# A new explicit order for the first phase of a windowed-attention and feed-forward kernel

## The chip, the cores and the metric

The kernel runs on one core of one Trainium2 chip. The metric is the device time of one execution in microseconds, lower is better. The kernel before has a median of 850.51 us over three runs (849.96 to 850.99). About 0.2% of that (1.7 us) is what a measurement of this kernel can tell from no change.

## The reference

Eight batches of eight heads attend over 576 positions of 64 elements, each position to itself and the 63 before it; the result, laid out as 4608 tokens of 512 elements, goes through a two-layer feed-forward net with a leaky rectifier.

```python
scores = scale * np.matmul(q, k.transpose(0, 1, 3, 2))
mask = (rel >= 0) & (rel < 64)              # rel = query position - key position
scores = np.where(mask, scores, -1e9) - rowmax
attn = np.exp(scores) / (sum + 1e-09)
x = np.matmul(attn, v)                      # to (4608, 512)
h = x @ w_in                                # (512, 2048)
g = np.maximum(0.01 * h, h)
out = g @ w_out                             # (2048, 512)
```

The weights arrive as 64-bit floats; everything else is 32 bits.

## The kernel before, in words

Each product of the feed-forward net is made of three matmuls: a value is split into a rounded high part and the low part that is left, and high by high, high by low and low by high are summed. Scores are made transposed, keys on the partitions, so the maximum of a row runs across partitions, and GpSimd makes it with a PARTITION_ALL_REDUCE (line 332).

The program has two parts. The first is a list of names, `ORDER`, ahead of its `|`: each name is one step, and each step issues its instructions on its own engine in the order of the list. No scheduler moves them, so the list is the order of every queue. Everything behind the `|`, and all later work, is arranged by a planner in the program that the change does not touch. What the names do, with the line of the profile of before:

- TensorE: `X6` is six idle matmuls (503). `S0` makes the scores of block pair 0, in two banks; for pairs from 1 on it first writes the mask into the banks with two matmuls (312), then 64 small matmuls (278). `Z0` adds the mask to bank 0 afterwards. `N0` subtracts the maximum of bank 0 (346), `V0` multiplies the exponentials by the values (367), `T0` transposes a result (393), `M0` is a first product of the feed-forward net (431), `W0` the second product of the same job (467).
- GpSimd: `P0` to `P15`, one maximum for each bank (332).
- VectorE: `E0` and `E1` copy scores and mask from a bank to SBUF (322); `sub4` and later subtract a maximum (337); `sm`, `rec`, `y` are the sum, its reciprocal and the normalised result (374, 379, 386); `L` is the low part of x (401), `gl` that of the rectified h (445). `bits`, `sign`, `clamp`, `join`, `rest` (225, 229, 237, 242, 251) turn one 64-bit weight tile n into a high and a low part, with `abs` and `chi` (233, 245) on ScalarE between them. `bits`, `sign`, `clamp`, `join`, `rest`, `sub` and `gl` read SBUF alone; `sm`, `y` and `L` read a matmul bank.
- ScalarE: `E2` and later copy scores out of a bank (324), `exp` (351, 353), `H` is the high part of x (397), `lk` and `gh` are the rectifier and its high part (436, 441).
- DMA: `q`, `k`, `v` load a block pair's input on SyncE's queue (163, 167, 174); `raw` loads a weight tile (210), the first three on SyncE's queue and the others on ScalarE's. Weight tiles have three buffers, so `raw3` waits for `join0`.

A maximum can start when its scores are in SBUF and, from `P4` on, when the `sub` before it has read the maximum before. `M0` to `M10` are the products of the first 512 tokens, and each needs the low parts of x (`L`) and of its own weights (`rest`); `M1` needs `rest2`, `M2` needs `rest4`, `M3` needs `L3`, `W10` needs `rest15`. From `M11` on the weights are made already.

These lines of the program run the list:

```python
order, late = ORDER.split("|")
for name in order.split():
    step(name)()
```

Of the kernel before, what the change touches and what calls it, by code (L numbers as in the profile page):

```python
# [53 lines left out]
ORDER = """
q0 X6 S0 k1 raw0 q1 E0 P0 E1 bits0 sign0 raw1 v0 q2 k2 P1 X3 Z0 Z1 S1 abs0 E2 N0 exp0 X1 N1 bits1 sign1 abs1 clamp0
join0 clamp1 V0 sm0 join1 exp1 V1 E3 S2 chi0 raw2 chi1 raw3 rec0 sm1 rec1 bits2 sign2 y1 y0 P2 P3 N2 raw4 E4 rest1
rest0 E5 exp2 N3 exp3 T0 v1 V2 V3 k3 q3 abs2 H0 S3 v2 v3 q4 k4 sm2 P4 sub4 P5 rec2 sm3 L0 y2 rec3 clamp2 y3 exp4 V4 E6
T1 join2 H1 sub5 sm4 bits3 rec4 L1 exp5 X4 V5 P6 raw5 chi2 sign3 abs3 E7 bits4 rest2 sub6 sm5 clamp3 rec5 y4 y5 sign4
P7 M0 lk0 exp6 gh0 M1 abs4 gl0 T2 W0 join3 sub7 bits5 clamp4 V6 lk1 H2 exp7 raw6 L2 gh1 join4 V7 S4 chi4 raw7 chi3 gl1
sm6 sign5 sm7 rest4 rec7 rec6 rest3 M2 E8 abs5 y7 y6 T3 bits6 sign6 W1 lk2 H3 L3 clamp5 P8 M3 gh2 gl2 join5 v4 k5 q5  # L60
E9 S5 v5 q6 k6 raw8 lk3 gh3 chi5 abs6 sub8 bits7 exp8 gl3 M4 lk4 rest5 sign7 clamp6 W2 V8 P9 abs7 sub9 join6 gh4 raw9
M5 bits8 gl4 E10 sm8 sign8 exp9 chi6 W3 P10 clamp7 rec8 y8 join7 rest6 lk5 abs8 clamp8 gh5 V9 M6 W4 gl5 join8 bits9
sub10 sm9 sign9 rec9 y9 raw10 E11 raw11 chi7 P11 chi8 lk6 exp10 T4 gh6 abs9 rest8 rest7 bits10 M7 V10 W5 gl6 sign10
clamp9 H4 abs10 sub11 join9 L4 bits11 sm10 rec10 clamp10 y10 join10 lk7 raw12 exp11 gh7 gl7 S6 V11 chi9 rest9 sign11
W6 chi10 raw13 abs11 E13 E12 P12 rest10 sm11 bits12 clamp11 join11 rec11 y11 chi11 raw14 sign12 abs12 bits13 sign13
clamp12 sub12 join12 M8 T5 v6 q7 v7 k7 W7 lk8 gh8 H5 exp12 abs13 chi12 raw15 gl8 P13 bits14 L5 V12 sign14 clamp13
rest11 sub13 sm12 join13 rest12 rec12 S7 y12 E14 raw16 abs14 exp13 clamp14 join14 bits15 P14 W8 V13 M9 sub14 sm13
sign15 chi14 E15 exp14 chi13 abs15 lk9 gh9 P15 rec13 y13 V14 T6 rest14 rest13 sub15 M10 sm14 clamp15 gl9 rec14 join15
y14 exp15 raw17 H6 chi15 V15 W9 bits16 sign16 L6 lk10 gh10 abs16 raw18 sm15 rec15 gl10 y15 T7 H7 rest15 W10 clamp16
bits17 join16 sign17 L7 abs17 clamp17 join17 bits18 raw19 chi16 ev0 chi17 ev1 raw20 rest16 sign18 abs18 rest17 M11  # L70
bits19 clamp18 M12 lk11 gh11 gl11 lk12 gh12 sign19 join18 M13 W11 M14 gl12 abs19 raw21 chi18 lk13 bits20 clamp19
join19 chi19 raw22 sign20 rest18 rest19 W12 M15 gh13 gl13 abs20 W13 bits21 clamp20 sign21 join20 bits22 abs21 lk14
sign22 clamp21 join21 raw23 chi20 M16 gh14 gl14 W14 rest20 raw24 abs22 clamp22 join22 chi21 raw25 bits23 rest21 sign23
bits24 lk15 chi22 gh15 gl15 sign24 abs23 abs24 clamp23 join23 bits25 chi23 raw26 lk16 M17 W15 clamp24 sign25 rest22
join24 M18 abs25 gh16 raw27 clamp25 gl16 rest23 join25 W16 chi24 rest24 bits26 sign26 lk17 chi25 rest25 raw28 abs26
gh17 bits27 clamp26 gl17 sign27 join26 abs27 clamp27 join27 chi26 lk18 chi27 gh18 bits28 sign28 rest26 gl18 k8 q8 v8
W17 q9
|
abs28 raw29 clamp28 join28 bits29 raw30 sign29 rest27 abs29 bits30 chi28 clamp29 sign30 rest28 abs30 join29 clamp30
raw31 chi29 bits31 sign31 rest29 abs31 join30 clamp31 chi30 join31 rest30 chi31 rest31  # L80
# [1346 lines left out]
```

## Time and profile before

| | |
|---|---|
| median of three runs | 850.51 us |
| the profiled execution | 850.4 us, of it 848.6 us from the first to the last instruction |
| TensorE busy over the span | 841.8 us (99%) |
| VectorE busy from 20 to 80 us | 19.54, 19.70 and 19.12 of each 20 us |
| end of the first phase | about 140 us, where the planner's attention begins |

Times in the profile are in microseconds from the first instruction. Matmuls are pipelined and their ends are modelled, so a matmul's row may end later than the next begins. VectorE's instructions overlap by some 0.08 us, so a step of 0.42 us takes some 0.34 us of the queue. A row of the chain or timeline gives start, duration, engine, line, what is written and read, and the idle time before it.

### The profile page before, as it was taken

The numbers are of one execution on the slowest core, as the hardware profiler recorded it, in microseconds if no ns is written. First come the engines' busy times: TensorE is split into PE (matmuls) and PEld (weight loads), VectorE is DVE, ScalarE is ACT, GpSimd is POOL, SyncE is SP. The second block draws the span as 40 slices with busy tenths as digits, with TensorE's granted clock in tenths as the row PEclk, the third lists the DMA queues.
The fourth block names the chain that finished last, engine by engine and source line by source line (L and its number), as shares of the span: only waits on it lengthen the run. The fifth ranks groups of instructions, "written<-read, shape, count | busy, mean of one in ns | idle before, by whom it ended". The sixth has DMA issues, their size and how long they took to land.

```text
span 848.6 us, 16788 instructions
## 1 busy us (share of the span) xinstructions
PE 841.8 (99%) x6778; PEld 686.3 (81%) x6778; DVE 620.1 (73%) x883; ACT 375.7 (44%) x605; POOL 383.3 (45%) x218
## 2 busy tenths in 40 slices
PE   8999999999999999999999999999999999999998
PEld 5887888888878888888888888888888888888886
DVE  6999885748768779867649987585679955446863
ACT  4665654333433354454444433443354533324431
POOL 5422000878888715587587757857111111111110
PEclk9999999999999999999999999999999999999999
DMA  9875756798899869999999999999998986777682
GB/s 324 273 233 155 253 162 235 264 284 271 288 307 323 301 212 286 314 305 317 333 351 358 365 351 318 365 310 311 242 272 235 238 248 196 198 198 198 193 211 92
DMA packets 127757, 226.80 MB, mean 267 GB/s; under 512 B 15552, under 2 KB 46400, under 8 KB 127680
## 3 DMA queue, kind: packets, MB, share of 16 engines
q0 software_dynamic: 51552, 90.18, 38.4%
q10 hardware_dynamic: 35664, 77.31, 27.9%
q1 hardware_dynamic: 40464, 58.24, 21.1%
q8 instruction: 53, 0.87, 0.4%
q14 instruction: 24, 0.20, 0.1%
HBM read 172.52 MB, written 53.06 MB: 266 GB/s over the span
## 4 chain that ended last, share of the span: by engine, by line
PE 97%; DVE 2%; DMA 0%; ACT 0%; issue 0%; ACTq 0%
PE m L1118 27%; PE z L1181 18%; PE acc L929 11%; PE h L920 11%; PE y L1138 10%; PE h L431 5%; PE acc L467 5%; PE s L278 4%; PE o L740 4%; PE o L367 1%; DMA qk<-qk 0%; PE t L393 0%; DVE raw L225 0%; PE s L312 0%; DVE w L242 0%; DVE raw L229 0%
## 5 line engine op out<-in xcount | busy, mean ns | idle before, releaser
L1118 PE MATMUL m<-pfew,p 128*128 128x512 f32 x720 | 169.4, 391 | 0.0
L1118 PEld LDWEIGHTS m<-pfew,p 128*128 128x128 f32 x720 | 134.5, 188 | 28.3
L1102 POOL DMA_DIRECT2D p<-w_first x42 | 31.8, 757 | 113.4 <-PE m L1118 61.0
L929 PE MATMUL acc<-p,gs 128*128 128x512 f32 x324 | 80.6, 394 | 0.0
L1127 DVE TENSOR_TENSOR p<-m,pxa 128x512 f32<-128x512 f32 x60 | 41.3, 689 | 47.0 <-PE m L1118 46.0
L681 POOL PARTITION_ALL_REDUCE g<-late_f x20 | 36.8, 1875 | 78.7 <-DVE late_f L666 72.0
L684 POOL PARTITION_ALL_REDUCE late_o<-late_f x20 | 66.1, 3329 | 12.2 <-ACT late_f L692 7.0
L1118 PE MATMUL m<-pxb,p 128*128 128x512 f32 x288 | 70.9, 391 | 0.0
L1130 ACT ACTIVATE p<-p 128x512 f32<-128x512 f32 x60 | 37.9, 631 | 73.6 <-DVE p L1127 73.5
L929 PEld LDWEIGHTS acc<-p,gs 128*128 128x128 f32 x324 | 59.8, 188 | 12.8
L1127 DVE TENSOR_TENSOR pxa<-m,pxa 128x512 f32<-128x512 f32 x60 | 41.4, 690 | 35.4 <-PE m L1118 34.7
L684 POOL PARTITION_ALL_REDUCE late_o<-e x18 | 59.5, 3336 | 8.5 <-ACT e L692 3.6
L1118 PEld LDWEIGHTS m<-pxb,p 128*128 128x128 f32 x288 | 53.7, 188 | 11.3
L684 POOL PARTITION_ALL_REDUCE late_o<-late_e x18 | 59.3, 3322 | 5.5 <-ACT late_e L692 5.2
L1181 PE MATMUL z<-gs,p 128*128 128x512 f32 x240 | 57.6, 389 | 0.0
L920 PE MATMUL h<-pxa,p 128*128 128x512 f32 x228 | 54.9, 390 | 0.0
L1102 POOL DMA_DIRECT2D p<-w_second x28 | 22.7, 811 | 68.5 <-PE z L1181 31.0
L1181 PEld LDWEIGHTS z<-gs,p 128*128 128x128 f32 x240 | 45.0, 188 | 9.4
L1181 PE MATMUL z<-third,p 128*128 128x512 f32 x216 | 51.9, 389 | 0.0
L1181 PE MATMUL z<-pxa,p 128*128 128x512 f32 x216 | 51.9, 389 | 0.0
L920 PEld LDWEIGHTS h<-pxa,p 128*128 128x128 f32 x228 | 42.7, 188 | 9.0
L1102 POOL DMA_DIRECT2D p<-w_sums x16 | 12.0, 747 | 80.2 <-PE z L1181 55.8
(193 smaller groups left out, 1775.3 us busy)
## 6 DMA issues: line engine op xcount, KB each, us to landing
p<-w_first POOLq DMA_DIRECT2D x42, 1024.0 KB, 6.9
p<-w_second POOLq DMA_DIRECT2D x28, 1024.0 KB, 8.3
p<-w_sums POOLq DMA_DIRECT2D x16, 1024.0 KB, 5.7
qk<-qk ACTq DMA_DIRECT2D x26, 512.0 KB, 5.8
pspare<-w_second ACTq DMA_DIRECT2D x16, 512.0 KB, 7.2
w_sums<-pspare ACTq DMA_DIRECT2D x16, 512.0 KB, 7.7
raw<-w_out ACTq DMA_DIRECT2D x15, 512.0 KB, 3.9
raw<-w_in ACTq DMA_DIRECT2D x14, 512.0 KB, 3.9
```

What stands on the lines that cost most here:

```text
L431: nc.tensor.matmul(ps, a[:, k, :], b[:, k, part], start=n == 0, stop=n == len(terms) - 1)
L467: nc.tensor.matmul(acc[c, i], a[:, ts], b, start=begin and n == 0, stop=end and n == 2)
L681: nc.gpsimd.partition_all_reduce(most_of(j), e_of(m)[:, j], P, ReduceOp.max)
L684: nc.gpsimd.partition_all_reduce(sum_of(j), e_of(m)[:, j], P, ReduceOp.add)
L920: nc.tensor.matmul(ps, a[:, k, :], b[:, k], start=i == 0, stop=i == len(terms) - 1)
L929: nc.tensor.matmul(acc[c, i], a[:, i * P : (i + 1) * P], b, start=begin and k == 0, stop=n in ends and k == 2)
L1102: nc.gpsimd.dma_start(to, of, max_dma_last_dim=2048)
L1118: nc.tensor.matmul(tiles[b], w[:, 256 * i + 128 * kt : 256 * i + 128 * kt + 128], x_part(OF_X[k], j, kt), start=begin and c == 0, stop=c = ...
L1127: nc.vector.tensor_tensor(to(), tiles[b], x(), ALU.add)
L1130: nc.scalar.activation(to(), to() if b is None else tiles[b], AF.Prelu, alpha=0.01)
L1138: nc.tensor.matmul(tiles[i], a, b, start=f == 0 and k == 0, stop=f == FT - 1 and k == 2)
L1181: nc.tensor.matmul(tiles[b + i], a, x, start=begin and f == 0 and c == 0, stop=f == half - 1 and c == 2, skip_group_check=not begin,)
```

## The change

All 515 names ahead of the `|` are the same, in another order; nothing is added or removed. The list becomes one text line shorter, so each line of the program moves up by one. On GpSimd only `P2` and `P3` change places. The list's beginning shows the kind of change:

```diff
-q0 X6 S0 k1 raw0 q1 E0 P0 E1 bits0 sign0 raw1 v0 q2 k2 P1 X3 Z0 Z1 S1 abs0 E2 N0 exp0 X1 N1 bits1 sign1 abs1 clamp0
-join0 clamp1 V0 sm0 join1 exp1 V1 E3 S2 chi0 raw2 chi1 raw3 rec0 sm1 rec1 bits2 sign2 y1 y0 P2 P3 N2 raw4 E4 rest1
...
+X3 X6 q0 raw0 S0 E0 bits0 E1 sign0 q1 raw1 k1 S1 bits1 abs0 sign1 E3 clamp0 abs1 Z0 raw2 E2 P0 P1 clamp1 join0 N0 exp0
+P3 v0 q2 Z1 N1 k3 exp1 join1 V0 k2 raw3 sm0 S2 P2 rec0 chi0 y0 rest0 V1 N3 bits2 E4 chi1 P4 N2 q3 sm1 v1 raw4 rec1 v2
...
```

Three places matter to what follows. The first is SyncE's queue at the start, before (`qk` is q or k of pairs 0 and 1 with line 163 for q and 167 for k; `raw` is a weight tile, `p_1` holds q and k of pairs 2 and 3):

```order
L163 DMA qk_83<-qk 128x512
L167 DMA qk_84<-qk 128x512
L210 DMA raw_146<-w_in 128x1024
L163 DMA qk_84<-qk 128x512
L210 DMA raw_154<-w_out 128x1024
L174 DMA v<-vW 128x2x520
L163 DMA p_1_78<-qk 128x512
L167 DMA p_1_78<-qk 128x512
```

And the same place after the change:

```order
L162 DMA qk_83<-qk 128x512
L209 DMA raw_115<-w_in 128x1024
L162 DMA qk_84<-qk 128x512
L209 DMA raw_156<-w_out 128x1024
L166 DMA qk_84<-qk 128x512
L209 DMA raw_202<-w_in 128x1024
L173 DMA v<-vW 128x2x520
L162 DMA p_1_78<-qk 128x512
```

`k1` moves from second to fifth place, behind both first weight tiles, and `raw2` moves ahead of `v0`.

The second place is VectorE's queue from its first score copy to where `clamp` and `join` of the first two weight tiles stand, before:

```order
L322 SCALAR_TENSOR_TENSOR e<-s_0_111,p_0_77 128x512
L322 SCALAR_TENSOR_TENSOR e<-s_1_112,p_0_77 128x512
L225 TENSOR_SCALAR raw_146<-raw_146 128x512
L229 SCALAR_TENSOR_TENSOR raw_146<-raw_146 128x512
L225 TENSOR_SCALAR raw_154<-raw_154 128x512
L229 SCALAR_TENSOR_TENSOR raw_154<-raw_154 128x512
L237 TENSOR_SCALAR raw_146<-raw_146 128x512
L242 SCALAR_TENSOR_TENSOR w_213<-raw_146 128x512
L237 TENSOR_SCALAR raw_154<-raw_154 128x512
L374 TENSOR_SCALAR sm_225<-o_216 128x4
L242 SCALAR_TENSOR_TENSOR w_227<-raw_154 128x512
```

After:

```order
L321 SCALAR_TENSOR_TENSOR e<-s_0_117,p_0_77 128x512
L224 TENSOR_SCALAR raw_115<-raw_115 128x512
L321 SCALAR_TENSOR_TENSOR e<-s_1_118,p_0_77 128x512
L228 SCALAR_TENSOR_TENSOR raw_115<-raw_115 128x512
L224 TENSOR_SCALAR raw_156<-raw_156 128x512
L228 SCALAR_TENSOR_TENSOR raw_156<-raw_156 128x512
L236 TENSOR_SCALAR raw_115<-raw_115 128x512
L236 TENSOR_SCALAR raw_156<-raw_156 128x512
L241 SCALAR_TENSOR_TENSOR w_208<-raw_115 128x512
L241 SCALAR_TENSOR_TENSOR w_219<-raw_156 128x512
L373 TENSOR_SCALAR sm_233<-o_221 128x4
```

`bits0` moves ahead of `E1`, both clamps ahead of both joins, and `sm0` behind them.

The third place is VectorE's queue behind `sub5`, beside GpSimd's `P6`, up to `rest2` and `sub6`, before:

```order
L374 TENSOR_SCALAR sm_408<-o_389 128x4
L225 TENSOR_SCALAR raw_281<-raw_281 128x512
L379 RECIPROCAL sm_408<-sm_408 128x4
L401 TENSOR_TENSOR pxa_13_332<-t_399,pxa_12_331 128x4x128
L229 SCALAR_TENSOR_TENSOR raw_281<-raw_281 128x512
L225 TENSOR_SCALAR raw_295<-raw_295 128x512
L251 TENSOR_TENSOR pfew_85<-w_404,pfew_85 128x512
L337 TENSOR_TENSOR e<-e,g 128x512
```

After:

```order
L241 SCALAR_TENSOR_TENSOR w_407<-raw_202 128x512
L400 TENSOR_TENSOR pxa_13_375<-t_384,pxa_12_374 128x4x128
L224 TENSOR_SCALAR raw_297<-raw_297 128x512
L228 SCALAR_TENSOR_TENSOR raw_231<-raw_231 128x512
L373 TENSOR_SCALAR sm_440<-o_389 128x4
L373 TENSOR_SCALAR sm_442<-o_413 128x4
L378 RECIPROCAL sm_442<-sm_442 128x4
L228 SCALAR_TENSOR_TENSOR raw_297<-raw_297 128x512
L250 TENSOR_TENSOR pfew_85<-w_407,pfew_85 128x512
L336 TENSOR_TENSOR e<-e,g 128x512
```

`join2` now stands behind `sub5` (it stood ahead of it), `bits3` has gone ahead of this stretch, and `sm5`, `rec5` and `sign4` have come ahead of `rest2`. On TensorE the list begins with nine idle matmuls in a row, `X3 X6`, where `X6` stood ahead of `S0` and `X3` behind it; `S1` follows `S0` at once, and `Z0` and `Z1`, which stood ahead of `S1`, now stand each just ahead of `N0` and `N1`; `S2` stands between `V0` and `V1`, and `X1` has gone to behind `V2`.

More of the change, by code (lines that the diff above doesn't have):

```diff
@@ L54 @@
 ORDER = """
-q0 X6 S0 k1 raw0 q1 E0 P0 E1 bits0 sign0 raw1 v0 q2 k2 P1 X3 Z0 Z1 S1 abs0 E2 N0 exp0 X1 N1 bits1 sign1 abs1 clamp0
-join0 clamp1 V0 sm0 join1 exp1 V1 E3 S2 chi0 raw2 chi1 raw3 rec0 sm1 rec1 bits2 sign2 y1 y0 P2 P3 N2 raw4 E4 rest1
-rest0 E5 exp2 N3 exp3 T0 v1 V2 V3 k3 q3 abs2 H0 S3 v2 v3 q4 k4 sm2 P4 sub4 P5 rec2 sm3 L0 y2 rec3 clamp2 y3 exp4 V4 E6
-T1 join2 H1 sub5 sm4 bits3 rec4 L1 exp5 X4 V5 P6 raw5 chi2 sign3 abs3 E7 bits4 rest2 sub6 sm5 clamp3 rec5 y4 y5 sign4
-P7 M0 lk0 exp6 gh0 M1 abs4 gl0 T2 W0 join3 sub7 bits5 clamp4 V6 lk1 H2 exp7 raw6 L2 gh1 join4 V7 S4 chi4 raw7 chi3 gl1
@@ L60 @@
[L60 to L74, printed above, removed]
@@ L75 @@
-join24 M18 abs25 gh16 raw27 clamp25 gl16 rest23 join25 W16 chi24 rest24 bits26 sign26 lk17 chi25 rest25 raw28 abs26
-gh17 bits27 clamp26 gl17 sign27 join26 abs27 clamp27 join27 chi26 lk18 chi27 gh18 bits28 sign28 rest26 gl18 k8 q8 v8
-W17 q9
+X3 X6 q0 raw0 S0 E0 bits0 E1 sign0 q1 raw1 k1 S1 bits1 abs0 sign1 E3 clamp0 abs1 Z0 raw2 E2 P0 P1 clamp1 join0 N0 exp0
+P3 v0 q2 Z1 N1 k3 exp1 join1 V0 k2 raw3 sm0 S2 P2 rec0 chi0 y0 rest0 V1 N3 bits2 E4 chi1 P4 N2 q3 sm1 v1 raw4 rec1 v2
+y1 exp3 sign2 T0 V3 exp2 V2 rest1 sub4 X1 bits3 sm3 sm2 S3 E5 H0 rec2 exp4 y2 rec3 y3 L0 T1 V4 abs2 X4 P5 clamp2 sub5
@@ new lines @@
+join2 H1 L1 bits4 exp5 V5 E6 q4 sign3 raw5 M0 sm4 sm5 P6 rec5 chi2 E7 sign4 abs3 rest2 sub6 v3 rec4 clamp3 lk0 M1 gh0
+y5 P7 abs4 y4 clamp4 join3 gl0 k4 sub7 T2 exp6 V6 join4 raw6 W0 sm6 H2 exp7 bits5 L2 lk1 V7 chi3 sign5 chi4 rec6 raw7
+y6 sm7 S4 rest4 gh1 rec7 abs5 gl1 q5 E8 y7 M2 T3 clamp5 rest3 W1 P8 bits6 join5 H3 v4 lk2 chi5 k5 L3 sub8 sign6 M3 gh2
+gl2 raw8 exp8 V8 E9 bits7 sign7 P9 S5 abs6 clamp6 join6 lk3 raw9 gh3 q6 sm8 rec8 chi6 abs7 rest5 sub9 gl3 bits8 M4
+sign8 clamp7 lk4 W2 exp9 E10 abs8 join7 M5 y8 P10 gh4 clamp8 W3 raw10 gl4 lk5 gh5 chi7 rest6 join8 raw11 sub10 V9
@@ new lines @@
+bits9 W4 k6 sign9 gl5 E11 sm9 abs9 v5 rec9 rest7 chi8 y9 exp10 P11 clamp9 bits10 M6 T4 join9 H4 lk6 V10 rest8 W5 chi9
+sign10 raw12 abs10 sm10 sub11 bits11 sign11 abs11 L4 gh6 clamp10 join10 exp11 chi10 rec10 M7 raw13 gl6 y10 q7 S6 V11
+clamp11 rest9 E12 P12 join11 sm11 v6 bits12 W6 lk7 rec11 sign12 y11 chi11 gh7 rest10 E13 T5 sub12 M8 raw14 H5 exp12
+gl7 k7 V12 abs12 rest11 bits13 sign13 W7 lk8 clamp12 join12 sm12 rec12 L5 abs13 raw15 clamp13 gh8 chi12 bits14 P13
+sub13 sign14 gl8 abs14 S7 W8 join13 exp13 clamp14 raw16 rest12 E14 join14 v7 y12 bits15 V13 sign15 sm13 M9 P14 rec13
@@ new lines @@
+raw17 sub14 chi13 chi14 E15 abs15 rest13 exp14 y13 clamp15 P15 rest14 V14 T6 bits16 lk9 H6 join15 sub15 sm14 bits17
+sign16 gh9 rec14 M10 y14 gl9 L6 exp15 raw18 V15 chi15 abs16 sm15 rec15 W9 clamp16 lk10 join16 gh10 y15 T7 gl10 rest15
+sign17 raw19 H7 bits18 abs17 chi16 L7 sign18 clamp17 W10 rest16 abs18 join17 clamp18 raw20 M11 join18 bits19 sign19
+M12 v8 chi17 ev1 chi18 rest17 lk11 gh11 raw21 M13 gl11 bits20 ev0 abs19 lk12 clamp19 join19 M14 raw22 sign20 chi19
+abs20 W11 bits21 gh12 gl12 rest19 sign21 rest18 abs21 clamp20 lk13 join20 W12 clamp21 bits22 join21 gh13 gl13 raw23
@@ L78 @@
+chi20 lk14 sign22 raw24 M15 chi21 abs22 W13 rest20 clamp22 gh14 join22 gl14 chi22 M16 raw25 lk15 bits23 rest21 sign23
+bits24 sign24 abs23 gh15 abs24 rest22 clamp23 clamp24 gl15 W14 join23 bits25 chi23 join24 rest23 raw26 W15 sign25
+raw27 lk16 abs25 M17 chi24 gh16 clamp25 join25 chi25 gl16 raw28 bits27 rest25 bits26 sign26 sign27 lk17 rest24 gh17
+gl17 abs26 q9 clamp26 M18 join26 abs27 W16 clamp27 q8 chi26 join27 bits28 lk18 gh18 chi27 sign28 k8 rest26 W17 gl18
 |
```

## The prediction

> **What bounds the kernel now.** I read the page's busy times first, then busy time by stretches of 20 us, then the timelines of each engine through the first 40 us.
>
> ```profile
> span 848.6 us, 16788 instructions
> PE 841.8 (99%) x6778; PEld 686.3 (81%) x6778; DVE 620.1 (73%) x883; ACT 375.7 (44%) x605; POOL 383.3 (45%) x218
> ```
>
> ```profile
> 0.00:20.00 20.00, 17.95 (x290) 11.47 (x291) 13.54 (x24) 9.52 (x17) 9.70 (x9) 1.00 0.92 333
> 20.00:40.00 20.00, 18.98 (x335) 15.72 (x336) 19.54 (x50) 12.97 (x27) 8.82 (x5) 1.00 0.85 268
> 40.00:60.00 20.00, 20.00 (x225) 16.25 (x218) 19.70 (x43) 13.86 (x27) 5.17 (x3) 1.00 0.73 224
> ```
>
> The columns of the second fence are stretch, length, then busy time of TensorE's matmuls, its weight loads, VectorE, ScalarE and GpSimd. TensorE is full from 40 us on. So a microsecond won or lost before about 40 us goes straight to the end, as long as the later work is never late; and almost nothing can be won after it. VectorE is also nearly full there, 19.5 and 19.7 of 20 us. Before 40 us what TensorE does and waits for is this:
>
> ```profile
> 1.45 2.93 PE L503 MATMUL idle<-p 128*128 128x512 f32 x6 [1.45 <-DVE p L514]
> 4.74 1.98 PE L278 MATMUL s<-qk 64*64 64x64 f32 x64 [0.37 <-DMA qk<-qk]
> 6.66 0.97 PE L503 MATMUL idle<-p 128*128 128x512 f32 x3
> 24.43 1.70 PE L431 MATMUL h<-pxa,pfew 128*128 128x256 f32 x12
> 26.60 1.69 PE L431 MATMUL h<-pxa,pfew 128*128 128x256 f32 x12 [0.47 <-ACT g L436]
> 33.05 1.96 PE L431 MATMUL h<-pxa,pfew 128*128 128x256 f32 x12
> 35.05 0.63 PE L393 MATMUL t<-unit,y 128*128 128x128 f32 x4
> 36.90 1.77 PE L431 MATMUL h<-pxa,pfew 128*128 128x256 f32 x12
> ```
>
> The last five rows are M0, M1, M2, T3 and M3. M2 lasts 1.96 where M1 takes 1.69: it stands still inside for a weight's low part. What TensorE needs there comes from VectorE:
>
> ```profile
> 32.84 0.67 DVE L251 TENSOR_TENSOR pfew<-w,pfew 128x512 fp32r<-128x512 f32 x1
> 34.17 0.74 DVE L386 TENSOR_TENSOR y<-o,sm 128x256 f32<-128x256 f32 x2
> 36.34 0.69 DVE L401 TENSOR_TENSOR pxa<-t,pxa 128x512 fp32r<-128x512 f32 x1 [0.19 <-ACT pxa L397]
> ```
>
> These are rest4 (done 33.51, M2 began at 33.05), y7 and y6 (done 34.91, T3 at 35.05), and L3 (done 37.03, M3 at 36.90). So **VectorE sets the pace up to M3**, and TensorE alone after it. I judge the change by when VectorE has L3.
>
> **What a maximum costs VectorE.** GpSimd's first six maxima and some of VectorE's steps from SBUF beside them:
>
> ```profile
> 7.57 1.99 POOL L332 PARTITION_ALL_REDUCE g<-e  x1 [7.12 <-DVE e L322]
> 9.47 2.06 POOL L332 PARTITION_ALL_REDUCE p<-e  x1
> 11.43 2.07 POOL L332 PARTITION_ALL_REDUCE p<-p  x1
> 13.92 1.78 POOL L332 PARTITION_ALL_REDUCE p<-p  x1 [0.42 <-ACT p L324]
> 17.16 1.78 POOL L332 PARTITION_ALL_REDUCE g<-e  x1 [1.45 <-ACT e L324]
> 20.18 2.00 POOL L332 PARTITION_ALL_REDUCE g<-e  x1 [1.25 <-DVE sm L374]
> ```
>
> ```profile
> 8.92 0.69 DVE L229 SCALAR_TENSOR_TENSOR raw<-raw 128x512 uint32<-128x512 uint32 x1
> 9.54 1.31 DVE L225 TENSOR_SCALAR raw<-raw 128x512 uint32<-128x512 uint32 x1
> 13.93 1.58 DVE L242 SCALAR_TENSOR_TENSOR w<-raw 128x512 uint32<-128x512 uint32 x1
> 15.77 0.40 DVE L225 TENSOR_SCALAR raw<-raw 128x512 uint32<-128x512 uint32 x1
> 19.34 0.68 DVE L337 TENSOR_TENSOR e<-e,g 128x512 f32<-128x512 f32 x1
> 24.03 0.87 DVE L229 SCALAR_TENSOR_TENSOR raw<-raw 128x512 uint32<-128x512 uint32 x1
> 24.82 0.56 DVE L225 TENSOR_SCALAR raw<-raw 128x512 uint32<-128x512 uint32 x1
> ```
>
> A `bits` takes 0.40 alone and 1.31 when it starts 0.07 into a maximum; a `join` takes 1.58 against the 0.69 of the `sign` of equal size. So a step that starts at a maximum's beginning loses 0.9 us. The `sign` at 8.92 started 1.35 into the maximum that began at 7.57 and lost nothing. I take the price as what is left of the first 0.9 us of the maximum. Grouped by line, the steps from SBUF in the first 20 us (count, then busy time and mean ns of one):
>
> ```profile
> L225 DVE TENSOR_SCALAR raw<-raw 128x512 uint32<-128x512 uint32 x3 | 2.6, 871 | 0.0
> L242 DVE SCALAR_TENSOR_TENSOR w<-raw 128x512 uint32<-128x512 uint32 x2 | 2.3, 1134 | 0.0
> L251 DVE TENSOR_TENSOR pfew<-w,pfew 128x512 fp32r<-128x512 f32 x2 | 1.9, 972 | 0.0
> L237 DVE TENSOR_SCALAR raw<-raw 128x512 f32<-128x512 f32 x2 | 1.7, 874 | 0.0
> ```
>
> With 0.40 for a `bits` or `clamp` and 0.69 for the others their collisions come to 3 x 0.47 + 2 x 0.44 + 2 x 0.28 + 2 x 0.47 = 3.8 us.
>
> The Trainium skill, "SBUF — State Buffer", section "Who interferes with whom", says the same pair of ports is shared and that who comes second blocks fully, until the whole instruction of the first has ended. Here the trace differs: the join at 13.93 ended at 15.51, and its maximum at 15.70. By that rule each collision would cost up to 2.1 us, by the rows 0.9.
>
> **Part one, up to sub4.** The start: `X3 X6` puts three more idle matmuls ahead of S0. Six took 2.93 (with one modelled end in it), so three more take between 0.97 (the row of three at 6.66) and 1.5; S0 could have begun at 4.38 but for its input's 0.37. S0 begins at 5.4 instead of 4.74, near the lower end since the six hold one long last row; VectorE's E0 follows it, and the first maximum begins at 7.57 + 0.65 = 8.2. In the new order the five maxima can run without a gap, where before 0.42 and 1.45 were lost ahead of the fourth and fifth. At 1.9 to 2.05 each (start to start 9.47 - 7.57 and 11.43 - 9.47, with 0.1 to 0.2 when a VectorE step gets the memory first), five end at 18.2 to 18.6, and sub4 can start at 18.6 instead of 19.34. Two things must hold for that. VectorE must be there: it did the same steps (all but one `sm`) in 19.34 - 6.78 = 12.6 us before, (E0 started at 6.78, 0.1 behind S0's last row), of which 3.8 were collisions. That leaves 8.8, so from 7.4 on it has 18.6 - 7.4 - 8.8 = 2.4 us to lose. I find 2.3 to 3: `sign0` and `sign2` 0.3 to 0.5 each, `clamp0` 0.5 to 0.9, `join0` and `rest0` up to 0.8 each. And the inputs must be there:
>
> ```profile
> 2.12 0.43 SPq L163 DMA_DIRECT2D qk<-qk  x1
> 3.25 0.67 SPq L174 DMA_DIRECT2D v<-vW  x1
> ```
>
> ```profile
> qk<-qk SPq DMA_DIRECT2D x1, 256.0 KB, 6.1
> v<-vW SPq DMA_DIRECT2D x1, 520.0 KB, 7.6
> ```
>
> Before, q1 landed at 2.12 + 6.1 = 8.2 and v0 at 3.25 + 7.6 = 10.85; between them 512 KB of raw1 and 520 KB of v0, so 390 KB a microsecond. Now k1 is the last input of S1 and has raw1 ahead of it: 8.2 + 512/390 = 9.5. S1's small matmuls began at 9.01 and now begin at 9.5 to 9.6, done by 10.6. Its banks then go through E3 in 0.6, and the third maximum does not begin before 12.3, so the lateness is covered by 1 us; without cover it would cost 0.5. v0 lands at 12.2 and k2 at about 14.1, V0 and S2 start at about 13 and 14: just in time. **Term: -0.7 at sub4, from -1.0 to +0.3** (no gain, and the S1 lateness not covered to half).
>
> **Part two, from sub4 to L3.** VectorE is full, so what counts is the work ahead of L3 and the collisions. Counted in the new list, `clamp5` and `join5` have come ahead of L3 and `sign6` has gone behind: +0.42 (a clamp by the `bits` row's size). At P6 before, `sign3` (0.87 at 24.03) and `bits4` (0.56 at 24.82) lost 0.3 together; now E6, the score copy for P6, stands behind exp5 on ScalarE, P6 starts some 0.3 later, and `bits4`, `sign3` or `sign4` stand at its beginning: 0 to 0.9, I take 0.5, so +0.2. The 0.19 for which L3 waited on ScalarE before goes, since y6 and y7 now come ahead of `rest3`: -0.2. **Term: +0.4, from -0.3 to +1.2.**
>
> **Part three, from M3 to the end.** TensorE runs full. What could be late is the last weight of the first 512 tokens:
>
> ```profile
> 84.86 2.99 PE L467 MATMUL acc<-p,gs 128*128 128x512 f32 x12
> 83.42 0.68 DVE L251 TENSOR_TENSOR p<-w,p 128x512 fp32r<-128x512 f32 x1
> ```
>
> That is W10 and rest15, done 0.76 before W10 began. In the new list `bits17`, `clamp16` and `join16` come ahead of rest15, 0.34 + 0.34 + 0.6 = 1.3 us more. Against that, the `gl` steps stand later in VectorE's list, so the waits in front of them go:
>
> ```profile
> 66.44 0.86 DVE L445 TENSOR_TENSOR gs<-g,gs 128x512 fp32r<-128x512 f32 x1 [0.58 <-ACT gs L441]
> ```
>
> That one waited 0.58. With rest15's spare 0.76 this covers the 1.3: **term 0, up to +0.5**. All later work keeps its order, and starts sooner or later as a whole.
>
> **Sum.** -0.7 + 0.4 + 0 = -0.3. The profiled execution took 850.4, 1.8 more than its span, and lies at the median of the runs shown (850.51). Forecast: **850.1 us**, no change that can be told; its own range 849.0 to 851.4.
>
> **The rivals.** *A, the clock.* TensorE's matmuls are at half speed at first: S0's 64 took 1.98 us, the idle matmuls behind it 0.97/3 = 0.32 each against 0.49 at 1.45. Nine idle matmuls without the 0.37 gap could bring full speed before S0; then S0 takes about 1 us, the maxima begin 0.6 earlier and so may sub4: 850.1 - 0.6 = 849.5. Against it: full speed came only at about 7 us, after five microseconds of nearly steady work. The Trainium skill, "TensorE: Matmul & The Clock Gate", section "What's actually happening", states about 3.4 us of sustained work, in a window that does not start with the kernel; by that S0 could be fast here. *B, collisions gather (slower).* Between sub5 and L3 three steps stand where a maximum may just have begun: `sign3` at P6, `clamp3` behind `rec4` at P7, `gl1` at P8. At 0.9 each they cost 2.7, against 0.5 at these places before; with the 0.4 of extra work and no gain in part one VectorE has L3 2.6 late, less the 0.2: 850.4 + 2.4 = 852.8; with two of them and the gain, 851.2. It decides from the second collision on. For it: `clamp3` follows `sub6` by one short step only. Against it: a step right behind a `sub` can slip in first, as the next maximum starts 0.16 after the `sub` ends (sub4 at 19.34 + 0.68, P5 at 20.18). *C, no collision.* The new places dodge all of P6 to P8: part two becomes 0.4 - 0.5 - 0.2 = -0.3, and with -1.0 in part one and the fast S0 of A 850.4 - 1.9 = 848.5. *D, given back.* The gain of 0.3 is lost at W10, where VectorE is 0.5 late: 850.6.
>
> **How the numbers follow.** Forecast 47%, A 13%, B 17% (a third of it within 0.2%), C 15%, D 8%. Faster by over 0.2% needs 848.8: C and the edge of A and of the forecast, 0.22. Slower needs 852.2: most of B and the forecast's edge, 0.16. Within 0.2%: 0.62. The range must reach to C's time and into B's: 848.3 to 852.1.
>
> **What would show it.** Right: S0 at about 5.4, the first maximum at 8.2, five maxima without gaps, sub4 at about 18.6, M3 at 36.4 to 36.9, no TensorE wait from there to 140 us. Wrong: S1 waiting for k1 well past 9.6, gaps between the first maxima; `sign3`, `clamp3` or `gl1` at 1.2 us or more (B); all VectorE steps between sub5 and L3 at their plain durations (C); TensorE idle at W10 (D).

## The result, and the profile after

The changed kernel takes **855.57 us** (median of five runs, 855.13 to 857.58) against 850.36 for the kernel before on the same chip. The ratio is 1.0065, with a 95% interval from 1.0054 to 1.0077: 5.2 us slower, where no change was forecast, and 3.5 us above the range. The profiled execution is the longest of the five, 857.58, and the only one whose granted clock is below 1.000 (0.998). Its span is 7.2 longer than the one before, so some two of these 7.2 us belong to that execution alone; the section on the hardware shows 1.5 of them.

The page of the changed kernel, span and busy times:

```profile
span 855.8 us, 16780 instructions
PE 843.8 (99%) x6778; PEld 687.7 (80%) x6778; DVE 622.7 (73%) x883; ACT 374.7 (44%) x605; POOL 383.9 (45%) x218
```

TensorE is busy 2.0 us longer than before (841.8), with the same 6778 matmuls, and idle 5.2 us longer. Where, the stretches of 20 us say (columns as before: stretch, length, busy time of matmuls, weight loads, VectorE, ScalarE, GpSimd, then the granted clock, the DMA share and GB/s):

```profile
0.00:20.00 20.00, 15.87 (x263) 10.33 (x265) 11.78 (x22) 8.38 (x15) 10.07 (x9) 1.00 0.90 318
20.00:40.00 20.00, 18.82 (x295) 15.01 (x292) 19.67 (x48) 13.16 (x27) 7.94 (x4) 1.00 0.80 253
40.00:60.00 20.00, 17.95 (x185) 14.39 (x184) 18.27 (x37) 11.38 (x23) 6.39 (x3) 0.91 0.71 229
80.00:100.00 20.00, 19.16 (x125) 15.45 (x122) 18.46 (x40) 13.15 (x24) 3.13 (x2) 1.00 0.60 190
```

TensorE is busy 2.1 us less than before in the first 20 us (15.87 against 17.95), and is no longer full from 40 to 60 and from 80 to 100 us, where it was full before. On TensorE's timeline the steps that answer to those shown before are S0, M0, M3, M4, and two that wait now, T4 and V15:

```profile
5.69 1.16 PE L277 MATMUL s<-qk 64*64 64x64 f32 x64
25.88 1.69 PE L430 MATMUL h<-pxa,pfew 128*128 128x256 f32 x12
38.93 1.97 PE L430 MATMUL h<-pxa,pfew 128*128 128x256 f32 x12
43.20 1.70 PE L430 MATMUL h<-pxa,pfew 128*128 128x256 f32 x12
56.28 0.94 PE L392 MATMUL t<-unit,y 128*128 128x128 f32 x4 [2.04 <-DVE y L385]
88.14 0.69 PE L366 MATMUL o<-p,e 128*64 128x65 f32 x16 [0.83 <-ACT raw L232]
```

M0 comes 1.45 us later than before (24.43), M3 2.03 later (36.90). M4 is 3.0 later, of which 0.6 is V8, which stands ahead of it now; by M5 the delay is 2.44. T4 waits 2.04 for y9, V15 waits 0.83. V15's row names ScalarE's `abs` (232), which V15 does not read; it writes the bank that y14 has to empty first, and y14 ended at 87.99, 0.15 before V15 began, as y9 ended 0.15 before T4. From M11 on the delay is 7.14 to the end. What T4 waits for is on VectorE:

```profile
51.40 0.69 DVE L241 SCALAR_TENSOR_TENSOR w<-raw 128x512 uint32<-128x512 uint32 x1 [1.46 <-DMA w_single<-w]
53.07 0.69 DVE L228 SCALAR_TENSOR_TENSOR raw<-raw 128x512 uint32<-128x512 uint32 x1
53.68 1.26 DVE L444 TENSOR_TENSOR gs<-g,gs 128x256 fp32r<-128x256 f32 x1
55.14 0.66 DVE L250 TENSOR_TENSOR pfew<-w,pfew 128x512 fp32r<-128x512 f32 x1
55.72 0.42 DVE L385 TENSOR_TENSOR y<-o,sm 128x256 f32<-128x256 f32 x1
```

The first row is join8. It waits 1.46 us for a store to memory of an earlier joined weight (line 246), whose SBUF tile it is to overwrite. Before, the same wait was 0.19:

```profile
47.91 0.69 DVE L242 SCALAR_TENSOR_TENSOR w<-raw 128x512 uint32<-128x512 uint32 x1 [0.19 <-DMA w_single<-w]
```

Behind it come, in the change, sign9, gl5 (which meets the beginning of P11, 1.26 instead of 0.42), rest7, and only then y9. Behind T4's wait the granted clock falls, which the section on the hardware shows.

### The profile page after: what moved, and what is told of

It reads as the page before. It is cut to its first block, busy times and chain, and to the rows that moved or that the text cites. A ratio compares the mean times of both kernels' runs of the same rounds, so it can differ in the third digit from the quotient of the medians.

```text
span 855.8 us, 16780 instructions
## 1 busy us (share of the span) xinstructions
PE 843.8 (99%) x6778; PEld 687.7 (80%) x6778; DVE 622.7 (73%) x883; ACT 374.7 (44%) x605; POOL 383.9 (45%) x218
## 4 chain that ended last, share of the span: by engine, by line
PE 91%; DVE 4%; DMA 3%; issue 0%; ACT 0%; ACTq 0%; SPq 0%; DVEq 0%
PE m L1117 27%; PE z L1180 18%; PE acc L928 11%; PE h L919 10%; PE y L1137 10%; PE s L277 4%; PE o L739 4%; PE acc L466 3%; PE h L430 3%; DMA p<-qk 1%; DMA raw<-w_out 1%; DMA w_single<-w 1%; DVE raw L228 1%; DMA p<-eye_mask 1%; PE o L366 1%; DVE w L241 1%
## 5 line engine op out<-in xcount | busy, mean ns | idle before, releaser
L331 POOL PARTITION_ALL_REDUCE g<-e x13 | 26.8, 2065 | 50.7 <-ACT e L323 39.7
```

## The experiments

All experiments are other orders of the same 515 names. Letters of theories are used anew from group to group. The delays at M0, M5, S6 and W10 are those of the profiled execution against the profiled execution of before; the times are medians, each beside its own runs of before (850.3 to 850.6).

| kernel | M0 | M5 | S6 | W10 | us, median | ratio, 95% interval |
|---|---|---|---|---|---|---|
| the change | 1.45 | 2.44 | 6.18 | 7.12 | 855.57 | 1.0054 to 1.0077 |
| a_then_b | 1.49 | 1.44 | 1.44 | 1.44 | 852.24 | 1.0010 to 1.0029 |
| a_then_b_M5 | 1.21 | 2.20 | 2.46 | 2.46 | 853.16 | 1.0019 to 1.0044 |
| b_then_a | -0.05 | 1.88 | 3.08 | 3.94 | 854.30 | 1.0029 to 1.0060 |
| b_loads | 2.31 | 1.84 | 1.84 | 1.84 | 851.98 | 1.0006 to 1.0029 |
| b_v1 | 1.38 | 0.89 | 0.89 | 1.21 | 851.30 | 1.0001 to 1.0022 |
| a_loads | 1.94 | 2.55 | 3.37 | 4.18 | 855.58 | 1.0039 to 1.0069 |
| a_v1 | 1.64 | 2.63 | 3.85 | 4.66 | 855.16 | 1.0047 to 1.0072 |
| a_loads_v1 | 1.12 | 2.10 | 2.87 | 3.71 | 856.25 | 1.0053 to 1.0083 |
| a_start | 0.64 | 1.76 | 3.34 | 4.22 | 855.56 | 1.0040 to 1.0066 |
| a_mid | 1.99 | 2.63 | 3.44 | 4.24 | 855.07 | 1.0042 to 1.0066 |
| a_join8 | 1.55 | 2.52 | 4.11 | 5.02 | 855.72 | 1.0051 to 1.0077 |
| a_join8_v8 | 1.95 | 2.55 | 4.12 | 4.92 | 855.80 | 1.0048 to 1.0073 |
| a_late | 2.12 | 2.73 | 5.47 | 6.46 | 857.25 | 1.0068 to 1.0094 |
| a_loads_v1_late | 1.67 | 2.66 | 5.08 | 6.35 | 857.59 | 1.0065 to 1.0089 |
| a_vq | 1.59 | 2.59 | 3.88 | 4.31 | 855.78 | 1.0047 to 1.0080 |
| a_v5 | 2.04 | 2.64 | 3.42 | 4.30 | 854.75 | 1.0043 to 1.0068 |
| a_fix | 0.71 | 1.86 | 6.21 | 6.23 | 855.64 | 1.0049 to 1.0074 |
| a_all | 3.16 | 4.30 | 4.27 | 5.95 | 854.47 | 1.0034 to 1.0061 |

Runs of one of these kernels lie up to 4.7 us apart, those of before up to 2.8, so single edits inside the changed order are judged by the traces first; medians that differ by less than 1 us are not told apart. A trace is one execution, and the same stretch of the same order differs between executions too, as some of the rows below show. Behind W17, the end of the list, the profiled executions of `a_then_b`, `b_loads`, `a_start`, `a_join8` and `a_vq` lose 1.1 to 3.1 us more, in a part of the program that no edit touches, so their profiled times are longer than the delays say.

### Where the loss sits: joints of the two orders

The first group cuts the list at M1 and joins one half of each, and exchanges the first twelve loads alone.

```diff
 b_loads: before, with
-q0 X6 S0 k1 raw0 q1 E0 ...
+q0 raw0 q1 raw1 k1 raw2 v0 q2 k3 k2 q3 v1 X6 S0 E0 ...
 a_loads: the change, with
-X3 X6 q0 raw0 S0 E0 ...
+q0 k1 raw0 q1 raw1 v0 q2 k2 raw2 v1 k3 q3 X3 X6 S0 E0 ...
 b_then_a: before up to M1, behind it what is left, in the change's order
 a_then_b: the change up to M1, behind it what is left, in before's order
```

> The changed order, with the first twelve loads on SyncE's queue in the order of before (q0 k1 raw0 q1 raw1 v0 q2 k2 raw2 v1 k3 q3); all else as in the change. Theory L (the loads): S1 waits 1.2 us for k1 and S2 1.0 us for k2, M0 is 1.45 us later than before, and that goes to the end: now 855.6 - 1.5 = 854.1 us (853.5 to 854.5), M0 at 24.4 or earlier. Theory F (the later waits, at T4 and V15, only follow from the late start): they go as well, 850.5 to 851.5. Theory M (all of the loss is made after M1): 855 to 855.6.

> The kernel before, with the first twelve loads on SyncE's queue in the order of the change (q0 raw0 q1 raw1 k1 raw2 v0 q2 k3 k2 q3 v1). Theory L: S1 and S2 come later by about 0.4 and 0.9 us, and 850.4 becomes 851.3 to 852.2. Theory F: the late start also brings later waits, 853 or more. Theory M: 850.4, the early slack covers it.

> The order of before up to and with M1 (26.6 us), then all remaining steps in the order of the change. Theories L and M: the later part makes its own losses, 2 us at T4, 0.6 to 1 us before S5, 0.9 us at V15, so 853 to 854.5. Theory F: with an early start they do not arise, 850.4 to 851.

> The order of the change up to and with M1, then all remaining steps in the order of before. Theory L: only the 1.45 us of the start are lost, 851.6 to 852.4. Theory F: the late start brings later waits with any order, 853.5 or more. Theory M: 850.4 to 851.

Measured: the change up to M1 costs 852.24 - 850.39 = 1.9 us, and before's order behind it adds no wait, for the delay stays at 1.44 to the end of the list. Before up to M1 with the change's rest costs 3.9. (Some of this belongs to the joint, where clamp4 waits 0.76 for abs4.) So the loss has two separate places, and the larger one lies behind M1. The loads of the change alone cost before 1.6 us, but the loads of before did not help the change: 855.58, with M0 at 26.37, where V4 now waits 0.90 for the third v load.

A cut at M5 splits the rest.

> The changed order up to M5, from there the steps that are left in the order of before. With the cut at M1 the same joint took 852.24. Theory L: M2 to M5 lose 0.4 to 1.0 us, and nothing is lost behind them: 852.6 to 853.3. Rival N (VectorE's list between M1 and M5 is the cause, and comes out later): 854.5 or more.

853.16, inside what was expected of theory L, and no wait behind the cut: 2.46 from S6 to the end. So **the start costs 1.9 us, M2 to M5 0.9 (1.0 by the delays, 1.21 to 2.20), and the part behind M5 2.4 in the median**. The 0.9 is less than medians tell apart and rests on the trace.

### The start

In the change V1 stands behind S2. One kernel puts it ahead again, one does the opposite to before, and one joins it to the loads:

```diff
 a_v1, and with the loads of before a_loads_v1: the change, with
-V0 k2 raw3 sm0 S2 P2 rec0 chi0 y0 rest0 V1 N3
+V0 k2 raw3 sm0 V1 S2 P2 rec0 chi0 y0 rest0 N3
 b_v1: before, with
-V0 sm0 join1 exp1 V1 E3 S2 chi0
+V0 sm0 join1 exp1 E3 S2 V1 chi0
```

> The changed order with one step moved: V1 stands ahead of S2 again (in the change it stands behind S2, and S2 stood still 0.96 us for its k). Theory V: V1 behind S2 holds two things, TensorE itself, which has no gap from 16.3 to 25.9 us in the changed kernel, and the third v load, which cannot be issued before V1 has read the buffer (17.41 us after, 14.12 before). Then V1 runs at about 13.7 instead of 16.7, that load is issued at about 14.4, the first product M0 comes 0.6 to 0.9 us earlier than 25.88, and the time is 854.7 to 855.0 against 855.57. Rival D: the loads fill their lane from 1 to 25 us without a gap, so the earlier v load only delays another one, and M0 stays within 0.3 us: 855.3 to 855.8.

> The kernel before with one step moved: V1 behind S2, as the change has it. The third v load was issued at 14.12 us, behind V1; now it goes out at about 16.5 and lands at about 22.3 instead of 19.9, and the second normalised row block comes 2.3 later too. Theory P: V4, at 21.33 before, waits for that load, and M0 comes 0.6 to 1.2 us later: 851.0 to 851.7. Rival: the loads have slack and nothing waits: 850.2 to 850.7.

> The changed order with its first twelve loads in the order of before and V1 ahead of S2: the two edits that each gained nothing alone, together. With the loads alone TensorE's wait of 0.96 us for k2 went, but V4 waited 0.9 us for the third v load, which V1 behind S2 held back; with V1 alone S2 and T1 waited. Theory P (one place, two inputs late; either alone covers the other): M0, at 25.88 us after the change, 26.07 and 26.37 in the two single edits, comes at 25.0 to 25.5, and the time is 854.4 to 855.0. Rival W (VectorE's own order in the start, L0 behind y2 and y3 above all, holds T1 and M0): M0 stays at 25.8 or later and the time at 855.1 to 855.6.

`b_v1` came out as expected, 851.30. SyncE's queue in before and in `b_v1`, the third v load:

```profile
14.12 0.55 SPq L174 DMA_DIRECT2D v<-vW  x1
```

```profile
15.73 0.55 SPq L174 DMA_DIRECT2D v<-vW  x1
```

And TensorE's V4 in `b_v1`:

```profile
22.71 0.69 PE L367 MATMUL o<-v,e 128*64 128x65 f32 x16 [1.34 <-DMA v<-vW]
```

The load cannot go out before V1 has read the buffer. It now goes out behind a weight tile, lands at 22.57 instead of 19.93, and V4 waits 1.34 us. This is shown: **V1 behind S2 costs before 1.0 us by itself** (0.1 to 1.9 by the interval). In the change, V1 ahead alone gained 0.4 (not told apart), since T1 then waits 0.84 for L0, which it waited 0.18 for in the change. With the loads of before as well, M0 came at 25.55, near the 25.0 to 25.5 of theory P; two of six runs took 854.16, the others 856.0 to 858.9, so the time says nothing. T1 then waited 0.65 for L0. The next kernel adds L0 right behind H0 and sub5 ahead of clamp2:

```diff
 a_start: a_loads_v1, with
-sub4 X1 bits3 sm3 sm2 S3 E5 H0 rec2 exp4 y2 rec3 y3 L0 T1 V4 abs2 X4 P5 clamp2 sub5
+sub4 X1 bits3 sm3 sm2 S3 E5 H0 L0 rec2 exp4 y2 rec3 y3 T1 V4 abs2 X4 P5 sub5 clamp2
```

> The changed order with the loads of before first, V1 ahead of S2, L0 right behind H0 and sub5 ahead of clamp2. Theory W (with the loads and V1 in place, T1 waited 0.8 us for L0 behind y2 and y3): M0 at 24.6 to 25.1 (24.43 before, 25.55 with the loads and V1 alone). The undisturbed runs with the loads and V1 alone took 854.16; this 853.3 to 853.9. Rival: M0 stays at 25.4 or later, 854.1 or more.

M0 at 25.07, as expected of W, and at 25.14 in `a_fix`, which begins alike: the delay at M0 falls from 1.45 to 0.64 and 0.71. So the order of the loads, V1 and L0, with sub5 that was not tried apart, make most of the start's loss in these two traces; a third one with this beginning, `a_all`, has M0 3.16 late, which the last section comes back to. The time did not fall (855.56): S6 is 3.34 late all the same, for T4 waits 1.43 ahead of it.

### M2 to M5

```diff
 a_mid: the change, with
-gl1 q5 E8 y7 M2 T3 clamp5 rest3 W1 P8 bits6 join5 H3 v4 lk2 chi5 k5 L3
+gl1 rest3 q5 E8 y7 M2 T3 clamp5 W1 P8 bits6 H3 v4 lk2 k5 L3 join5 chi5
```

> The changed order with rest3 behind gl1 (it stood at the beginning of P8 and took 1.53 us) and join5 and chi5 behind L3. Theory C (that collision and join5 hold W1 and M3, which stand still inside: 2.06 us for a W1 of 1.56, 1.97 for an M3 of 1.70): rest3 takes 0.7, W1 and M3 their plain times, M4 comes 0.5 to 0.8 us earlier than 43.20, and the time is 854.7 to 855.1, if nothing behind it takes the gain back. Rival: another step now stands at the beginning of P8, L3 stays late, and the time is 855.3 to 855.8.

rest3 in the change, which holds W1, and VectorE around P8 in `a_mid` (rest3, clamp5, bits6, L3; y7 is left out):

```profile
36.06 1.53 DVE L250 TENSOR_TENSOR pfew<-w,pfew 128x512 fp32r<-128x512 f32 x1
```

```profile
35.55 0.69 DVE L250 TENSOR_TENSOR pfew<-w,pfew 128x512 fp32r<-128x512 f32 x1
36.49 0.93 DVE L236 TENSOR_SCALAR raw<-raw 128x512 f32<-128x512 f32 x1
37.34 1.03 DVE L224 TENSOR_SCALAR raw<-raw 128x512 uint32<-128x512 uint32 x1
38.29 0.67 DVE L400 TENSOR_TENSOR pxa<-t,pxa 128x512 fp32r<-128x512 f32 x1
```

rest3 takes 0.69, and from M0 to M3 the delay falls by 0.25, where in the change it grows by 0.58: 0.8 us gained there. But clamp5 and bits6 now meet the maximum's beginning and lose 0.5 and 0.6, and at M5 only 0.35 of the gain is left (2.63 - 1.99 = 0.64, against 0.99). M4 came at 43.48, not 0.5 to 0.8 earlier than 43.20: the rival's outcome, though the median, 855.07, lies inside what was expected of C and cannot be told from the change. The collision is real; moving one step hands it to the next.

### Behind M5

First the wait at T4 was attacked by moving join8, with the steps that hang on it, and the v8 load by its place near raw17:

```diff
 a_join8: the change, with
-rest6 join8 raw11 sub10 ... rest7 chi8 y9 exp10 P11
+rest6 sub10 ... rest7 y9 join8 raw11 chi8 exp10 P11
 a_join8_v8: also v8 from behind M12 to behind gl18
 a_late: the change, with join8 behind T4, raw11 and chi8 behind lk6, bits17 and sign16 behind y14
 a_loads_v1_late: a_late and a_loads_v1 in one
```

> The changed order with join8, raw11 and chi8 moved to right behind y9, where T4 is not behind them. Theory L (TensorE's wait of 2.0 us at T4 is VectorE standing at join8 for the store of the sixth weight's single tile): the wait at T4 falls to 0.3 or less and the time falls by 1.2 to 2.0, to 853.5 to 854.4, and runs of 857 do not come. Rival N (the later loss is spread over VectorE's collisions and full list, and the named waits only show where it comes out): TensorE waits at the next transposition or at M7 instead, and the time is 855.0 or more.

> As the kernel with join8 behind y9, and the v8 load moved from behind M12 to behind gl18, where it can no longer share the lane with raw17. Theory L: V15 waited some 0.9 us for raw17's landing; that goes too, so 0.7 to 0.9 us less than with join8 alone: 852.7 to 853.6. Rival N: the same as with join8 alone, within 0.3.

> The changed order with five steps of its later part moved: join8 to behind T4, raw11 and chi8 to behind lk6, bits17 and sign16 to behind y14. Theory Q (TensorE waits at T4 or V10 and at V15 because on VectorE and ScalarE the steps that it needs, y9, exp10 and y14, stand behind steps that wait for a store or a load or are not needed yet): the wait at T4 or V10 falls from 1.4 to 2.0 us to at most 0.5 and the one at V15 from 0.4 to 0.9 to 0; 853.4 to 854.4. The earlier join8 edit, which only exchanged the wait at T4 for one of 1.4 at V10 since chi8 then stood ahead of exp10, is undone by this on ScalarE too. Rival N (VectorE's list is too full there in whatever order): a later product waits instead, 855.0 or more.

> Both of the two kernels before it in one. If P and Q hold their gains add: 852.6 to 853.6. If only Q holds: 853.4 to 854.2. If neither: 855 and more.

All four missed: 855.72, 855.80, 857.25, 857.59. In `a_join8` T4 no longer waits, but V10 waits 1.4 for exp10, which stood behind chi8, which waits for join8. The v8 load made no difference. In `a_late` neither T4 nor V10 waits, and S6 does:

```profile
61.94 1.18 PE L311 MATMUL s<-away,unit 128*128 128x512 f32 x2 [1.93 <-DVE pxb L400]
```

VectorE ahead of that (bits11, then the L4 that S6 waits for):

```profile
60.04 0.43 DVE L224 TENSOR_SCALAR raw<-raw 128x512 uint32<-128x512 uint32 x1 [1.37 <-DMA raw<-w_out]
61.11 0.68 DVE L400 TENSOR_TENSOR pxb<-t,pxb 128x512 fp32r<-128x512 f32 x1
```

With raw11 later, its landing is later, and L4 stands behind bits11, which waits for it. So y9, exp10 and L4, which TensorE needs next, all stand behind steps on the weights, and any of these that waits for a transfer passes its wait on. Two theories were left: the order on VectorE alone, or the transfers.

```diff
 a_vq: the change, moves on VectorE (and abs11): sm9 rec9 y9 right behind V9; L4 ahead of bits11 sign11; y14 ahead of bits17 sign16
 a_fix: a_vq, a_mid and a_start in one
```

> The changed order with moves on VectorE alone in its later part (abs11, which reads sign11, goes with it): sm9, rec9 and y9 right behind V9, ahead of bits9, sign9, gl5 and rest7; L4 ahead of bits11 and sign11; bits17 and sign16 behind y14. Loads, stores and join8 stay. Theory O (what TensorE waits for, y9, L4 and y14, stands behind steps on VectorE that nobody needs yet): the waits at T4 (1.0 to 2.0 us) and V15 (0.4 to 0.9) go, and none takes their place: 853.2 to 854.2 against 855.57. Theory S (the weight pipeline of three buffers with its loads and stores sets the pace there, the lane being full from 44 to 52 us): a wait of 1 us or more stays at V10, S6 or M7, 855.0 or more.

> The three kernels before it in one: the start, the middle and the later part. If all three theories hold, the parts add to 850.2 to 851.8, level with before. If S holds instead of O, 852.3 to 853.5.

855.78 and 855.64: theory O, the order on VectorE alone, falls. `a_vq` has theory S's outcome, and `a_fix` lies above both of its ranges. The waits at T4 and V15 did go, and one at V10 took their place, in TensorE's waits of `a_vq` (total, times, longest):

```profile
PE o L366 <- ACT e L352: 1.2, 1, 1.2
```

and of `a_fix`, which came to V10 earlier and waited longer:

```profile
PE o L367 <- ACT e L353: 3.3, 2, 2.8
```

In the change and in `a_v1`, `a_join8`, `a_vq`, `a_start` and `a_fix` V10 starts between 55.5 and 57.2 us, with M5 anywhere from 45.6 to 46.4: something else than TensorE's own pace sets it. In five of them V10 begins 5.4 to 5.8 us behind join8, through exp10 or T4; in `a_join8` join8 waits for nothing, and its own new place, behind y9, does it. How join8 reaches TensorE can be read from the seven traces that have the change's steps behind M5 unaltered on VectorE. The wait of join8 for the store, then the wait of T4:

| kernel | join8 | T4 |
|---|---|---|
| the change | 1.46 | 2.04 |
| a_start | 0.84 | 1.43 |
| b_then_a | 0.46 | 1.05 |
| a_v1 | 0.44 | 1.02 |
| a_loads | 0.04 | 0.62 |
| a_loads_v1 | 0.03 | 0.63 |
| a_mid | 0.03 | 0.62 |

T4's wait is join8's wait plus 0.6 in each. So it has two parts: 0.6 us that VectorE's order makes even when the store is in time, and what a late store adds.

What makes the store late in the change? One candidate is v5. SyncE's queue in before (v5, q6, k6) and in the change (q6, k6, v5, q7):

```profile
31.41 0.55 SPq L174 DMA_DIRECT2D p<-vW  x1
33.21 0.33 SPq L163 DMA_DIRECT2D qk<-qk  x1
39.79 0.33 SPq L167 DMA_DIRECT2D qk<-qk  x1
```

```profile
35.30 0.33 SPq L162 DMA_DIRECT2D qk<-qk  x1
42.83 0.33 SPq L166 DMA_DIRECT2D qk<-qk  x1
43.25 1.19 SPq L173 DMA_DIRECT2D p<-vW  x1
44.54 0.55 SPq L162 DMA_DIRECT2D qk<-qk  x1
```

The change puts v5 behind q6 and k6. k6 has to wait for its buffer until 42.83, and v5 with it. So its 520 KB fall into the same microseconds as raw9 (issued at 43.93), the store (44.34) and q7, and the store lands at 51.31 instead of 47.81.

```diff
 a_v5: the change, with v5 ahead of q6
 a_all: a_start, a_vq and a_v5 in one, and exp10 behind E11, ahead of abs9 and chi8
```

> The changed order with one load moved: v5 ahead of q6 and k6 on SyncE's queue, as before has it. In the change it stands behind k6, goes out at 43.25 us instead of 31.41 and shares the lane with the ninth weight tile, q7 and the store of the sixth weight's single, which then lands at 51.3 instead of 47.8; join8 waits for that store, and y9, chi8 and exp10 stand behind join8. Theory S' (the lane from 43 to 52 us, filled by v5's place): v5 goes out at 33 to 34, the store lands before 49.9, join8 waits for nothing, the wait at T4 falls from 1.0 to 2.0 us to 0.3 to 0.7, and the time is 854.0 to 854.8 against 855.57, without runs of 857. Rival: the lane is full in any order, the store lands after 50.3 as now, 855.2 or more.

> All that the runs point to together: the loads of before first, V1 ahead of S2, L0 behind H0 and sub5 ahead of clamp2 (start); v5 ahead of q6; y9 and L4 and y14 ahead of the VectorE steps that nobody needs yet; and exp10 behind E11, ahead of abs9 and chi8, for which it waited 1.2 us in the VectorE-only kernel. If the lane and the order on VectorE and ScalarE are together the cause of the 2.4 us behind M5: no TensorE wait of 0.4 or more from M5 to W10, the shift at W10 equals that at M5 (1.8 to 2.2 us), and the time is 852.0 to 852.9. If not, a wait of 1 us or more is left at T4, V10 or S6: 853.5 or more.

`a_v5` came out as theory S' expected, on SyncE's queue (v5), VectorE (join8, no wait) and TensorE (T4):

```profile
33.62 0.55 SPq L173 DMA_DIRECT2D p<-vW  x1
```

```profile
50.18 0.69 DVE L241 SCALAR_TENSOR_TENSOR w<-raw 128x512 uint32<-128x512 uint32 x1
```

```profile
55.07 0.63 PE L392 MATMUL t<-unit,y 128*128 128x128 f32 x4 [0.63 <-DVE y L385]
```

The store lands at 49.74, T4 waits 0.63 instead of 2.04, and the median is 854.75 (854.0 to 854.8 expected), though one run of five took 856.73. But this does not show that v5 was the cause. `a_mid`, `a_loads` and `a_loads_v1` leave v5 behind k6, and their traces say the same; `a_mid` (v5, T4):

```profile
43.53 1.54 SPq L173 DMA_DIRECT2D p<-vW  x1
55.04 0.63 PE L392 MATMUL t<-unit,y 128*128 128x128 f32 x4 [0.62 <-DVE y L385]
```

Its store landed at 49.47, those of the other two at 49.65 and 49.23. Over the traces that show its landing the store took 3.9 to 5.7 us from issue to landing where v5 goes out early (seven traces), and 4.9 to 7.4 where it stands behind k6 (twelve). So an early v5 seems to help, but the two ranges overlap, and neither the trace of `a_v5` nor its median can be told from the change's order by this.

In `a_all` T4 and V10 wait for nothing, and the delay at S6, 4.27, equals that at M5, 4.30. The late start of this execution is not what hid the wait at V10: exp10 was done at 54.23, ahead even of the 54.92 at which before begins V10, where in `a_fix` it was done at 56.88. So **the order on VectorE and ScalarE, with v5 early, accounts for the loss from M5 to S6**; `a_all` does not say what v5 had in it. Its median, 854.47, misses 852.0 to 852.9. V11, the next one, waits:

```profile
PE o L367 <- DVE y L386: 1.0, 1, 1.0
```

That is y10, behind gl6 on VectorE. With the rest up to W10 the delay grew by 1.7, and W10 itself takes 3.46 us instead of 2.99, with a wait for rest15 inside. What a complete repair of the part behind S6 would need stays open. No kernel of these beats the kernel before.

## Why the prediction was wrong

**The start, S0 to the first maximum: S0 nearly as forecast, the first maximum better, and worth nothing.** S0 began at 5.69 (5.4 forecast). It took 1.16 us instead of 1.98: in this execution the matmuls were at full speed by then, so rival A's mechanism, given 13%, did happen, and P0 began at 7.70 instead of 8.2. That was luck of the execution. Ten traces, the change's among them, have the change's first twelve loads and its order up to S1, and S0 takes 1.16 in two of them and 1.27 to 1.99 in the others; P0 begins anywhere from 7.47 to 8.84. What the start gave was lost behind it.

**"V0 and S2 start at about 13 and 14: just in time" failed.** This is the step of the sum that the -0.7 at sub4 rested on. S1's last input was priced rightly (k1 landed at 9.37, 9.5 forecast, and E3 hid it). k2 landed at 15.56, not at 14.1, and TensorE's waits show both:

```profile
PE s L277 <- DMA qk<-qk: 1.2, 1, 1.2
PE s L277 <- DMA p<-qk: 1.0, 1, 1.0
```

The fifth maximum, P4, had a gap of 1.74 ahead of it, for its scores come from S2, and sub4 came at 19.64, 0.3 late instead of 0.7 early. In seven of the ten traces k2 lands at 15.4 to 15.7; in the other three it lands at 14.2, as forecast, and sub4 still comes at 19.4: S0 was slow in two of them, and S2 stood still for 0.7 in the third, which its trace does not explain. So the gain needed a fast S0 and an early k2 together, and no trace has that with an undisturbed S2. Behind sub4 the sum left out V1: S2 now stands between V0 and V1, and it never asked what V1 holds. V1 holds the third v load (`b_v1`: 1.0 us).

**"VectorE sets the pace up to M3" failed from S2 to M0.** In the change TensorE has one idle gap of 0.18 us between 16.3 and 25.9 us. It lost another 1.15 us between sub4 and M0 to its own late start, which a sum over VectorE cannot see.

**Part two, +0.4 with an upper end of +1.2, was mis-sized:** from sub4 to M3 the change lost 2.03 - 0.30 = 1.7. The price of a collision was right for a step at a maximum's beginning (rest3 0.84 too long at P8, sign7 1.51 at P9), and too low for one that comes a little later: gl5 began 0.48 into P11 and still lost 0.84, where "what is left of the first 0.9" gives 0.4. Rival B was right that collisions gather, but not at the three places that it named: sign3 took 0.69, clamp3 0.40 and gl1 0.40, free of P6 to P8. The middle, M2 to M5, costs 0.9 to 1.0.

**Part three, "term 0, up to +0.5", was the largest miss: 2.4 us.** The step behind it, "all later work keeps its order", is false for M3 to W10: that stretch of the list is reordered too. I priced only the last weight, rest15 at W10, and in the change nothing waits there; it does, for some 0.5 us, where the earlier waits are gone (`a_vq`, `a_all`). The waits are at T4 and V15, whose inputs y9 and y14 moved behind weight steps on VectorE: T4 waits 0.6 us when the store for which join8 waits is in time, and as much more as join8 waits for it. That y9 and y14 moved is shown as the cause, for the waits go when they are put ahead (`a_vq`). Why the store lands late in some executions stays open; v5, moved behind k6 on SyncE's queue, fits and is not shown. The rule to count the queue that a step is moved past was kept for the first eight loads and not for the others.

The chance of slower, 0.16, was therefore worked out from one engine and one stretch. The sign said to watch, "gaps between the first maxima", did appear; "TensorE idle at W10" did not, and the waits that took its place were at T4, 36 us earlier, and at V15.

## What to carry to other kernels

A new order has to be read on every queue and up to where it ends: for each load that moves, see what it stands behind, and which buffer that one waits for. Then take each instruction at which the bound engine could wait, and list what has come ahead of its input on the engine that makes it; steps that nobody needs yet are harmless only as long as none of them waits for a transfer. When an edit removes a wait and the time stays, compare when the next consumer starts: if it starts at the same time whatever was moved, something else than that engine's pace sets it. And before an edit is given credit for a wait that fell, see how far that wait varies in the traces without the edit: T4's fell from 2.04 to 0.63 with v5 moved, and to 0.62 in traces where v5 stayed.
